# Two steps of an attention schedule in another order: the low parts of the next keys, and the weighted sums of a pair of heads

## The chip, the cores and the metric

The kernel runs on one core of one Trainium2 chip. The time is that of one launch in device microseconds (us), the median of several runs. The core's engines are called by their names in the profile: PE (TensorE, matrix products), DVE (VectorE), ACT (ScalarE), POOL (GpSimd) and SP (SyncE, which here only issues DMAs). Each of them works through its own list of instructions in order.

## The reference, cut to what matters

Three layers follow each other, and each takes the output of the one before.

```
scores = q k^T / 8                      # 4 batches x 8 heads, 576 tokens, head size 64, fp32
scores = where(block_i >= block_j, scores, -1e9)      # blocks of 64 tokens
attn   = exp(scores - rowmax);  attn /= rowsum
x      = attn v                         # then (2304 tokens, 512)

e      = argmax(x w_gate + bias[modality])            # 8 experts
x      = gate * relu(x w1[e]) w2[e]                   # 512 -> 1024 -> 512

h      = x w_in                                       # 512 -> 2048
out    = where(h >= 1, h, where(h <= -1, 0, (h+1)^2/4)) w_out
```

Everything is fp32 to a tight tolerance. A product is therefore made of several with 32-bit operands in a high and a low part: high is the rounded value, low is what the rounding left.

## The kernel before, in words

The work lies in three stretches: attention (to about 225 us of the span), experts (to about 450 us), the last layer (the rest). The change concerns attention alone.

Attention goes over 16 pairs of heads, n = 0 to 15; pair n is two heads of batch n // 4. For a pair there are seven kinds of score tiles, by rows of queries and by heads (`kinds`, line 312): kind 0 and 1 hold both heads, kinds 2 to 5 one head each, kind 6 the last 64 rows of both. A pair is seven steps, z = 0 to 6, and `orders` gives the kind of each step: for the pairs 1 to 14 the kinds 3, 1, 0, 4, 2, 6, 5, for pair 0 the kinds 2, 4, 0, 1, 5, 6, 3, and for pair 15 the kinds 3, 1, 4, 2, 6, 0, 5. The third step is z = 2, the fourth z = 3.

What a step puts into the engines' lists is written out by hand in the loop at lines 510 to 539, in this order:

- what `PLAN` has for (z, 0);
- `scores`: PE makes one tile of scores in PSUM;
- what `PLAN` has for (z, 1);
- `flip`: PE turns the exponentials of the step two before (LAG = 2), piece by piece, into a PSUM tile `pt`, and for most kinds ACT copies it to `pT` (line 388);
- `soft`: DVE takes the row maximum of the scores (lines 348, 353, 357), ACT takes the exponential with its row sum (line 359);
- DVE copies the turned tiles that ACT doesn't (kinds 1 and 6, line 523);
- what `PLAN` has for (z, 2).

The words in `PLAN`, which `act` (line 478) reads:

- "q", "k": PE turns the next pair's queries or keys into PSUM (`psq`, `psk`). For the keys DVE copies 128 columns to `kT` (line 291) and ACT writes the high parts `kd` (line 293, two instructions); POOL doubles them (line 295).
- "low": DVE computes the low parts `kl` of those keys from `psk` and `kd` (line 489, two instructions, called low below).
- a pair of numbers: `weigh`, PE's weighted sums of the values of the previous pair for these key tiles (line 402, `px`). "first": those of the first 64 rows (line 417, `py`), where for odd n - 1 DVE also lays out the row factors (lines 438 and 444), and ACT copies `py` to `xT` (line 421). "store": ACT copies `px` to `xT` (line 407), and for odd n - 1 the rows of that pair of pairs are put on the list `todo`.
- "rows": one entry of `todo`: PE turns finished rows back and multiplies them with the gate (line 454, `xr`), DVE scales them (lines 460 and 464), SP writes them to DRAM.
- "sum": DVE's reciprocal of the row sums (lines 426 and 427).

PSUM is shared: `psq`, `psk` and the scores of kind 6 use one tile ("big", one buffer), so kind 6 of a pair can be started when low has read `psk`. The turned tiles `pt`, the tile `py` and a tile `rkp` of the routing use two buffers in turn ("pt"). In the last two pairs the routing of the first 13 row tiles is woven in, up to three DVE instructions or small groups per step (lines 529 to 531).

```
PLAN = {(1, 0): ["rows", "q"], (2, 0): ["sum"], (2, 2): ["k", (0, 3)], (3, 0): ["rows"], (3, 2): ["low"],
        (4, 2): [(3, 5)], (5, 0): ["first"], (5, 1): ["store"], (6, 2): ["rows"]}
```

Of the kernel before, what the change touches and what calls it, by code (L numbers as in the profile page):

```python
# [49 lines left out]


ORDER_FIRST, ORDER_LAST, ORDER = (2, 4, 0, 1, 5, 6, 3), (3, 1, 4, 2, 6, 0, 5), (3, 1, 0, 4, 2, 6, 5)
PLAN = {(1, 0): ["rows", "q"], (2, 0): ["sum"], (2, 2): ["k", (0, 3)], (3, 0): ["rows"], (3, 2): ["low"],
        (4, 2): [(3, 5)], (5, 0): ["first"], (5, 1): ["store"], (6, 2): ["rows"]}
FROM = 0, 128, 256, 320, 448
LAG = 2
COPY = 4
# [64 lines left out]
def attention(late, weights, tc, q, k, v, ids, w_gate, mbias, x_dram, dram, ident, tabs):  # L122
# [355 lines left out]
    def act(n, z, at):  # L478

        if n >= B * NP:  # L480
            return
        for what in PLAN.get((z, at), ()):
            if what == "q" and n + 1 < B * NP:
# [1109 lines left out]
```

## Time and profile before

| | |
|---|---|
| median of 3 runs | 844.05 us (843.9 to 845.23) |
| the profiled execution | 843.12 us, span of its instructions 841.3 us |
| PE busy | 811.1 us (96% of the span) |
| DVE busy | 587.3 us (70%) |
| ACT busy | 474.9 us (56%) |
| POOL busy | 203.8 us (24%) |
| granted TensorE clock | 1.000 in the mean |

All shares are over the whole span, and the three stretches differ: from 240 us on PE is busy in every slice, and the chain of waits that ended last is nothing but PE there. In attention PE is busy for 18.0 to 19.0 of every 20 us between 40 and 180 us, and the other engines are far busier than in the rest.

### The profile page before, as it was taken

To read this page: it belongs to the slowest core of one execution; us is meant where nothing else is said; L and a number is where in the kernel's file an instruction comes from. 1 tells how busy PE (TensorE), PEld (TensorE's weight loads), DVE (VectorE), ACT (ScalarE), POOL (GpSimd) and SP (SyncE) were. 2 spreads that over 40 slices of the span, in tenths; PEclk is the share of its full clock that TensorE was granted. 3 is DMA by queue.
4 is the path that set the end of the run, shared out by engine and by line. 5 is a ranking of instruction groups with operands and counts; after the bars stand their busy time and mean duration, and the time that the engine had idled before them with its cause. 6 is when DMAs were issued, how large, how long until landed. Compare 5 with 4: busy or idle time off the path is not lost. (4 is left out here: it accounts for less than half of the span.)

```text
span 841.3 us, 13981 instructions
## 1 busy us (share of the span) xinstructions
PE 811.1 (96%) x4936; PEld 703.1 (84%) x4936; DVE 587.3 (70%) x1085; ACT 474.9 (56%) x964; POOL 203.8 (24%) x309
## 2 busy tenths in 40 slices
PE   6999999998899999999999999999999999999998
PEld 5676767766788888888888999999999988888887
DVE  6676666769666746787873766766636777777774
ACT  5867767766633434555543667666657644444442
POOL 8546455465411212120202000110000011112120
PEclk9999999999999999999999999999999999999999
DMA  6545646541654447665634453554634643333301
GB/s 144 133 123 136 169 123 160 144 100 36 214 169 125 168 121 236 224 202 163 194 115 138 142 175 125 170 180 145 206 123 161 226 147 137 126 125 126 129 35 38
DMA packets 138058, 123.17 MB, mean 146 GB/s; under 512 B 70183, under 2 KB 122423, under 8 KB 135296
## 3 DMA queue, kind: packets, MB, share of 16 engines
q1 hardware_dynamic: 132256, 107.98, 41.8%
q0 software_dynamic: 4384, 13.92, 4.8%
q8 instruction: 40, 0.66, 0.3%
q10 hardware_dynamic: 1344, 0.33, 0.2%
q14 instruction: 34, 0.28, 0.1%
HBM read 89.17 MB, written 40.37 MB: 154 GB/s over the span
## 5 line engine op out<-in xcount | busy, mean ns | idle before, releaser
L1031 PE MATMUL h<-yhi,wi 128*128 128x384 f32 x768 | 200.5, 338 | 1.1 <-ACTq L1265 1.1
L1031 PEld LDWEIGHTS h<-yhi,wi 128*128 128x128 f32 x768 | 139.6, 188 | 1.6 <-ACTq L1265 1.6
L1031 PE MATMUL h<-ylo,wi 128*128 128x384 f32 x384 | 129.2, 336 | 0.0
L359 ACT ACTIVATE pall<-s,nmax 128x384 f32<-128x384 f32 (+2 forms) x144 | 80.1, 568 | 51.2 <-DVE nmax L357 46.7
L1305 ACT ACTIVATE cl<-h,half 128x384 f32<-128x384 f32 x96 | 55.7, 581 | 69.5 <-PE h L1031 69.2
L1309 DVE SCALAR_TENSOR_TENSOR gg<-cl,h 128x384 f32<-128x384 f32 x96 | 52.2, 551 | 51.7 <-ACT cl L1306 49.7
L1435 PE MATMUL p<-wo,s 128*128 128x256 f32 (+1 forms) x432 | 87.8, 339 | 0.0
L1435 PEld LDWEIGHTS p<-wo,s 128*128 128x128 f32 x432 | 68.5, 188 | 9.2
L1490 POOL DMA_INDIRECT out_dram<-rest,tab x16 | 27.3, 1705 | 190.6 <-DVE rest L1457 185.0
L1031 PEld LDWEIGHTS h<-ylo,wi 128*128 128x128 f32 x384 | 72.1, 188 | 0.0
L377 PE MATMUL pt<-ident,pall 128*128 128x128 f32 x400 | 65.1, 281 | 3.8 <-DVE pT L523 1.8
L1435 PE MATMUL p<-wo,a 128*128 128x256 f32 (+1 forms) x330 | 66.0, 335 | 0.0
L1031 PE MATMUL h<-xhi,wh 128*128 128x512 f32 (+2 forms) x164 | 63.1, 385 | 0.0
L1031 PE MATMUL h<-xhi,wl 128*128 128x512 f32 (+2 forms) x164 | 61.6, 376 | 0.5 <-DVE wl L1115 0.5
L1031 PE MATMUL h<-xlo,wh 128*128 128x512 f32 (+2 forms) x164 | 61.6, 375 | 0.0
L1140 PE MATMUL acc<-wh,hl 128*128 128x512 f32 x152 | 59.6, 392 | 0.2 <-DVE hl L1129 0.2
L1435 PEld LDWEIGHTS p<-wo,a 128*128 128x128 f32 x330 | 52.8, 188 | 8.0
L1140 PE MATMUL acc<-wl,hh 128*128 128x512 f32 x152 | 59.3, 390 | 0.0
L1140 PE MATMUL acc<-wh,hh 128*128 128x512 f32 x152 | 59.1, 389 | 0.0
L357 DVE TENSOR_REDUCE nmax<-s 128x1 f32<-128x384 f32 (+1 forms) x64 | 39.7, 621 | 24.1 <-PE s L338 23.2
L1306 ACT ACTIVATE cl<-cl 128x384 f32<-128x384 f32 x96 | 50.5, 526 | 3.0
L1115 DVE TENSOR_TENSOR wl<-raw,wh 128x1024 fp32r<-128x1024 f32 x40 | 48.8, 1220 | 0.8 <-issue 0.8
(322 smaller groups left out, 1766.2 us busy)
## 6 DMA issues: line engine op xcount, KB each, us to landing
raw<-in_moe_w_dram SPq DMA_DIRECT2D x80, 256.0 KB
g_dram<-gg SPq DMA_DIRECT2D x48, 384.0 KB
g<-g_dram SPq DMA_DIRECT2D x18, 1024.0 KB
wi_raw<-in_moe_w_in_dram SPq DMA_DIRECT2D x16, 512.0 KB
wo_raw<-in_moe_w_out_dram SPq DMA_DIRECT2D x16, 512.0 KB
yr<-y_dram SPq DMA_DIRECT2D x18, 256.0 KB
x_dram<-xrow SPq DMA_DIRECT2D x33, 128.0 KB
v<-in_v_dram SPq DMA_DIRECT2D x32, 128.0 KB
```

The source lines that it names most:

```text
L357: nc.vector.tensor_reduce(nm[:, x:x + 1], pss, axis=AX.X, op=ALU.max, negate=True)
L359: nc.scalar.activation(pall[n % 2][:, o:o + w], pss[:, u:u + w], AF.Exp, bias=nm[:, x:x + 1], scale=1.0, accum_out=ssum[:, b, c, x:x + 1])
L377: nc.tensor.transpose(pt[:, kk, :], pa[:, o + kk * P:o + (kk + 1) * P], ident)
L1031: nc.tensor.matmul(ps, a[za], b[zb], start=(i == 0), stop=(i == n - 1))
L1115: nc.vector.tensor_tensor(wl, weights.raw.pop((s, f)), wh.bitcast(F32), op=ALU.subtract)
L1140: nc.tensor.matmul(accs[s][u], a[:, us], b[:, 1, :], start=(f == 0 and i == 0), stop=(f == NF - 1 and i == 2))
L1305: nc.scalar.activation(cl, ph, AF.Relu, bias=half, scale=0.5)
L1306: nc.scalar.activation(cl, cl, AF.Square)
L1309: nc.vector.scalar_tensor_tensor(gg[:, :, f % 2, :], cl.rearrange(t3, t=P), 1.0, ph.rearrange(t3, t=P), op0=ALU.min, op1=ALU.max)
L1435: nc.tensor.matmul(o, a, b, start=(x == 0 and i in FRESH), stop=(x == len(terms) - 1), skip_group_check=True)
L1490: outs.append(nc.gpsimd.indirect_dma_start(out=out[:, :], out_offset=bass.IndirectOffsetOnAxis(ap=tabs.tab[:, j, 0:1].bitcast(U32), axis=0 ...
```

## The change

One table is changed. Low moves from the end of the fourth step to its head, ahead of the scores and the softmax of that step. The weighted sums, which were made in three places (key tiles 0 to 2 at the end of the third step, 3 and 4 at the end of the fifth, the first 64 rows at the head of the sixth), now all stand at the end of the third step. The copies to `xT` follow at the fourth step rather than the sixth, and one of the "rows" moves from the head of the fourth step to the head of the fifth. No instruction is added or taken away.

```
-PLAN = {(1, 0): ["rows", "q"], (2, 0): ["sum"], (2, 2): ["k", (0, 3)], (3, 0): ["rows"], (3, 2): ["low"],
-        (4, 2): [(3, 5)], (5, 0): ["first"], (5, 1): ["store"], (6, 2): ["rows"]}
+PLAN = {(1, 0): ["rows", "q"], (2, 0): ["sum"], (2, 2): ["k", (0, 5), "first"], (3, 0): ["low"], (3, 1): ["store"],
+        (4, 0): ["rows"], (6, 2): ["rows"]}
```

In the lists below a name carries its pair: `s7_4` is the score tile of pair 7 and kind 4, `nmax7` its row maxima, `kl8` the low parts of the keys of pair 8, `xr` and `xrow` belong to "rows", and the last number only tells instances apart.

DVE, from the third to the sixth step of pair 7, before:

```order
L353 TENSOR_REDUCE nmax7_1488<-s7_0_1549 128x2
L291 COPY kT8_1568<-psk8_1562 128x128
L460 TENSOR_TENSOR xrow6_0_1590<-xr6_0_1587,rt_165 128x256
L464 TENSOR_TENSOR lg_166<-xr6_0_1587,rt_165 128x32
L357 TENSOR_REDUCE nmax7_1488<-s7_4_1594 128x1
L523 COPY pT7_1553<-pt7_1_0_1598 128x2x2x128
L489 TENSOR_TENSOR kl8_1570<-psk8_1562,kd8_1569 64x576 x2
L357 TENSOR_REDUCE nmax7_1488<-s7_2_1608 128x1
L348 TENSOR_REDUCE nmax7_1488<-s7_6_1626 128x1
```

and now:

```order
L353 TENSOR_REDUCE nmax7_1495<-s7_0_1556 128x2
L291 COPY kT8_1575<-psk8_1569 128x128
L489 TENSOR_TENSOR kl8_1577<-psk8_1569,kd8_1576 64x576 x2
L357 TENSOR_REDUCE nmax7_1495<-s7_4_1604 128x1
L523 COPY pT7_1560<-pt7_1_0_1609 128x2x2x128
L460 TENSOR_TENSOR xrow7_0_1620<-xr7_0_1617,rt_165 128x256
L464 TENSOR_TENSOR lg_166<-xr7_0_1617,rt_165 128x32
L357 TENSOR_REDUCE nmax7_1495<-s7_2_1624 128x1
L348 TENSOR_REDUCE nmax7_1495<-s7_6_1634 128x1
```

Low (line 489) now stands ahead of the maximum of kind 4, and the scaling of the rows behind it.

DVE in pair 0, whose fourth step is kind 1, before:

```order
L353 TENSOR_REDUCE nmax0_249<-s0_0_285 128x2
L291 COPY kT1_304<-psk1_298 128x128
L353 TENSOR_REDUCE nmax0_249<-s0_1_316 128x2
L489 TENSOR_TENSOR kl1_306<-psk1_298,kd1_305 64x576 x2
L357 TENSOR_REDUCE nmax0_249<-s0_5_333 128x1
```

and now:

```order
L353 TENSOR_REDUCE nmax0_249<-s0_0_285 128x2
L291 COPY kT1_304<-psk1_298 128x128
L489 TENSOR_TENSOR kl1_306<-psk1_298,kd1_305 64x576 x2
L353 TENSOR_REDUCE nmax0_249<-s0_1_318 128x2
L357 TENSOR_REDUCE nmax0_249<-s0_5_333 128x1
```

Here nothing but low and the maximum of kind 1 change places.

ACT in pair 14, from the third step to the sixth, before:

```order
L293 CAST kd15_2827<-psk15_2820 64x576 x2
L359 ACTIVATE pall0_157,ssum_163<-s14_4_2841,nmax14_2749 128x512
L388 COPY pT14_2810<-pt14_0_0_2877 128x2x128
L359 ACTIVATE pall0_157,ssum_163<-s14_2_2873,nmax14_2749 128x384
L421 COPY xT_162<-py13_2890 128x64
L407 COPY xT_162<-px13_2834 128x512
```

and now:

```order
L293 CAST kd15_2827<-psk15_2820 64x576 x2
L421 COPY xT_162<-py13_2845 128x64
L407 COPY xT_162<-px13_2834 128x512
L359 ACTIVATE pall0_157,ssum_163<-s14_4_2855,nmax14_2749 128x512
L388 COPY pT14_2810<-pt14_0_0_2897 128x2x128
L359 ACTIVATE pall0_157,ssum_163<-s14_2_2893,nmax14_2749 128x384
```

The two copies to `xT` now come right behind the high parts of the keys.

## Rows read from the trace of the kernel before

**Rows 1.** Page, part 2: granted clock in 40 slices, tenths of full speed

```profile
PEclk9999999999999999999999999999999999999999
```

**Rows 2.** Waits of PE, 0 to 240 us: us in total, times, longest

```profile
PE s L325 <- DVE kl L489: 15.4, 15, 1.8
```

**Rows 3.** Timeline of PE, kind 6 of pair 5: start, us, engine, line, count, idle before

```profile
84.36 0.40 PE L325 MATMUL s<-kd,qa 128*128 128x288 f32 x1 [0.99 <-DVE kl L489]
```

**Rows 4.** Timeline of PE, pair 7, fourth to seventh step

```profile
106.02 0.76 PE L454 MATMUL xr<-rh,xT 128*128 128x144 f32 x4
106.52 0.49 PE L335 MATMUL s<-kd,qa 128*128 128x512 f32 x1
...
108.34 0.66 PE L402 MATMUL px<-pT,v 128*64 128x192 f32 x8
108.83 0.29 PE L417 MATMUL py<-pT,v 128*64 128x64 f32 x4
110.10 0.40 PE L325 MATMUL s<-kd,qa 128*128 128x288 f32 x1 [0.99 <-DVE kl L489]
...
111.95 0.52 PE L377 MATMUL pt<-ident,pall 128*128 128x128 f32 x3
```

**Rows 5.** Timeline of DVE, pair 7, fourth and fifth step

```profile
106.82 0.42 DVE L460 TENSOR_TENSOR xrow<-xr,rt 128x256 f32<-128x256 f32 x1 [2.69 <-DMA q<-qc]
...
107.33 0.69 DVE L357 TENSOR_REDUCE nmax<-s 128x1 f32<-128x512 f32 x1
107.94 0.68 DVE L523 COPY pT<-pt 128x512 f32<-128x512 f32 x1
108.53 1.51 DVE L489 TENSOR_TENSOR kl<-psk,kd 64x576 fp32r<-64x576 f32 x2
110.08 0.56 DVE L357 TENSOR_REDUCE nmax<-s 128x1 f32<-128x384 f32 x1
```

**Rows 6.** Timeline of ACT, from the keys of pair 8 to those of pair 9

```profile
105.07 1.29 ACT L293 CAST kd<-psk 64x576 fp32r<-64x576 f32 x2
...
110.67 0.58 ACT L359 ACTIVATE pall<-s,nmax 128x384 f32<-128x384 f32 x1 [1.58 <-DVE nmax L357]
...
111.24 0.20 ACT L421 COPY xT<-py 128x64 f32<-128x64 f32 x1
...
111.81 0.61 ACT L388 COPY pT<-pt 128x512 f32<-128x512 f32 x1
...
114.95 0.65 ACT L252 ACTIVATE qT<-psq 128x576 f32<-128x576 f32 x1 [0.19 <-PE psq L183]
115.93 0.58 ACT L388 COPY pT<-pt 128x512 f32<-128x512 f32 x1 [0.33 <-PE pt L377]
...
118.37 1.29 ACT L293 CAST kd<-psk 64x576 fp32r<-64x576 f32 x2
```

**Rows 7.** Timeline of POOL and DVE, pair 8

```profile
116.92 2.33 POOL L262 TENSOR_TENSOR qa<-qT,qa 64x448 fp32r<-64x448 f32 x2
...
123.49 0.39 DVE L438 COPY rt<-rinv 64x16 f32<-64x16 f32 x2
```

**Rows 8.** Line 426 over the whole program: ns min/median/max, first and last start

```profile
L426 DVE TENSOR_SCALAR rinv<-ssum x8: 164/172/244, 38.4 to 222.1; 128x18 f32<-128x18 f32 x8
```

**Rows 9.** Timeline of pair 0: low, the last exponential of kind 1, its turning

```profile
18.85 1.52 DVE L489 TENSOR_TENSOR kl<-psk,kd 64x576 fp32r<-64x576 f32 x2 [0.60 <-ACT kd L293]
...
19.78 0.47 ACT L359 ACTIVATE pall<-s,nmax 128x256 f32<-128x256 f32 x1
...
21.39 0.60 PE L377 MATMUL pt<-ident,pall 128*128 128x128 f32 x4
```

**Rows 10.** Timeline of pair 14: the routing's tile, the high parts, the turning of kind 6

```profile
198.76 0.56 PE L686 MATMUL rkp<-oh,ones 128*128 128x104 bf16 x13 [0.21 <-DVE oh L678]
...
199.14 1.28 ACT L293 CAST kd<-psk 64x576 fp32r<-64x576 f32 x2
...
205.83 0.77 PE L377 MATMUL pt<-ident,pall 128*128 128x128 f32 x5 [0.54 <-ACT pall L359]
```

## The prediction

> **What bounds the kernel now.** I read the clock first: the granted share stands at nine tenths or more in all 40 slices [rows 1], which is the 2.4 GHz level, so durations can be carried from one place to another. Then the waits of PE over attention. One entry stands out: PE waits for low 15 times, 15.4 us in all, at most 1.8 [rows 2]. In the timeline that wait is 0.99 us before the first product of kind 6 in pair 5 and again in pair 7 [rows 3, 4], and 15 of them are the pairs 0 to 14, each of which prepares the keys of a next pair. The longest is that of pair 0; the other 14 share 15.4 - 1.8 = 13.6, 0.97 each.
>
> Why it waits: kind 6 needs the PSUM tile that holds the next keys, and low is the last to read it. In pair 7 low runs from 108.53 to 110.04 [rows 5], although all that it needs, the high parts, is there at 105.07 + 1.29 = 106.36 [rows 6]. In between DVE does the rows of the step, the maximum of kind 4 and a copy. So the wait is one of order on DVE, and everywhere else in these steps PE goes from one instruction to the next. Attention is PE plus this wait: two pairs take 110.10 - 84.36 = 25.74 us, 12.87 per pair, of which 11.88 is PE's own work [rows 3, 4].
>
> **The change part by part.** No instruction comes or goes, so each term is a wait.
>
> *Pairs 1 to 13, low earlier.* Low would begin at 106.40, when ACT's second high part is done, and give the tile free at 106.40 + 1.55 = 107.95 (1.55 is from its start to that of the next DVE instruction, 108.53 to 110.08 [rows 5]). PE has the same work as before between the keys and kind 6, only in another order, so it gets there at 110.10 - 0.99 = 109.11 [rows 4]. That is 1.16 us after the tile is free: the whole wait goes, 13 x 0.99 = 12.9 us. On SP the loads of values, which wait for the last weighted sum, come earlier by the same move, and nothing is queued behind them that was not before.
>
> *What is late next.* Behind low on DVE now stand the maximum of kind 4, the copy of a turned tile, the rows and the maximum of kind 2. With the sums moved ahead, PE begins kind 4 at 106.02 + (108.83 - 108.34) + 0.29 = 106.80 [rows 4] and DVE could take its maximum 0.81 later (106.52 to 107.33 [rows 4, 5]), at 107.61; low holds DVE until 107.95. Then 0.61 for the maximum, 0.59 for the copy (108.53 - 107.94), 0.51 for the rows (107.33 - 106.82), 0.59 from the maximum of kind 2 to its exponential (110.67 - 110.08) [rows 5, 6]: the exponential begins at 110.25 and ends at 110.83. PE wants it for turning kind 2 at 111.95 - 0.99 = 110.96 [rows 4]. The cover is 0.13 us, so a little will show.
>
> It can become more, since this is a ring: high parts on ACT, low, the two maxima, the exponential of kind 2, and ACT's way to the next high parts. From the start of the high parts to low it is 1.33, then 1.55 + 0.61 + 0.59 + 0.51 + 0.59 = 3.85, so 5.18. ACT's way from that exponential to the next high parts is 118.37 - 110.67 = 7.70; the two copies to xT (0.57, 111.24 to 111.81) leave it, which gives 7.13, and 0.52 of that is idle, waiting for PE (0.19 and 0.33), which gives 6.61 [rows 6]. The ring is 11.79 to 12.31 against PE's 11.88: from nothing to 0.43 us per pair, to 5.6 us in 13 pairs. I take 0.12, near the lower end, because both idle pieces wait for PE, and PE will come sooner: 1.6 us.
>
> *Row factors beside POOL.* In the pairs 2, 4, ... 12 four short DVE copies (lines 438 and 444) move from the sixth step, where POOL is done, to the third. There POOL does two subtractions, 116.92 to 119.25 in pair 8 [rows 7]. The copies take some 0.7 us (two are 0.39 [rows 7]); unhindered they are over 1.4 us before low can begin. If DVE and POOL shut each other out, each copy would get its turn only between two of POOL's instructions, the second after 119.25 and the last about 0.9 later; low would begin 0.5 late, 3.0 us in six pairs. Line 426, a short DVE instruction that runs while POOL works, takes 164 ns at best, 172 in the middle and 244 at worst [rows 8], so there is something, but small. I take 0.15 us in six pairs, 0.9 us, between nothing and 3.0. The Trainium skill, "SBUF — State Buffer", Who interferes with whom, says that a DVE copy in a two-port mode and a GpSimd instruction keep each other out for the whole of an instruction, whoever came first. By that rule the upper end holds; the spread of line 426 speaks for the rule and against its full price.
>
> *Pair 0.* Here low already waits for the high parts: 0.60 idle, released by ACT [rows 9]. It can't begin before 18.85, so the wait of 1.8 stays. But the maximum of kind 1, which ran before it, now comes after, at 18.85 + 1.55 = 20.40, and takes 0.69 as the other 512-wide one [rows 5]; two exponentials of 0.47 [rows 9] end at 22.07, and PE wants to turn kind 1 at 21.39 [rows 9]. That is 0.7 us late, and the exponential of kind 5 behind it adds about 0.2: a loss of 0.9 us (0 to 1.3, as PE has some slack later or not).
>
> *Pair 14 and the end of attention.* py now holds the buffer that the routing's tile rkp wants next, and ACT frees it only behind the high parts: 199.14 + 1.28 + 0.20 = 200.62, where PE began rkp at 198.76 [rows 10, 6]. That is a new wait of 1.9 us in PE's list, and low, the maxima and the routing queue behind it on DVE. It stands in for this pair's wait for low (under 1.0); followed to the turning of kind 6 (205.83, which waited 0.54 for ACT [rows 10]) I make it 1.2 later than before. About 0.7 comes back: one of the "rows" (0.50, 106.02 to 106.52 [rows 4]) is now done within the pairs and not between the first expert products, and pair 15 has its sums in one place. Net loss 0.5 us, from a gain of 0.7 to a loss of 1.9. Everything after 225 us hangs on this end alone and moves with it.
>
> *Sum.* -12.9 + 1.6 + 0.9 + 0.9 + 0.5 = -9.0 us. On the profiled execution, 843.12, this is 834.1; that execution lies 0.9 below the median of the runs, 844.05, from which it is 835.0. I take 834.5. All ends at their best give -13.6, all at their worst -1.1.
>
> **The rivals.**
> - *The maxima become the bound.* The ring is 12.31, since ACT keeps its idle pieces: -12.9 + 5.6 + 0.9 + 0.9 + 0.5 = -5.0, 838.6. For it: a cover of 0.13 us is no cover. Against it: both idle pieces wait for PE. 14%.
> - *Row factors shut out by POOL*, at full price: -12.9 + 1.6 + 3.0 + 0.9 + 0.5 = -6.9, 836.7. For it the 244 ns, against it the median of 172. 9%.
> - *All 15 waits go* and nothing takes their place: -15.4, 828.2. Against it are pair 0, where low is not held by order, and pair 14. 7%.
> - *It doesn't do what it says*: what PE saves in a pair is waited for elsewhere, or lost at the end of attention, where the weights of the first expert are fetched. 843.5. Against it: PE's other waits in attention are single ones. 6%.
> - *Slower.* The same ring, decided on ACT: if its way from the exponential to the high parts stays 7.70 although two copies left it, because DVE and PE pace it, the ring is 5.18 + 7.70 = 12.88, as long as a pair now. From there every further delay is a loss: with the row factors (3.0) and the pairs 0 and 14 (1.4) it is +4.4, 848. For it: low stands ahead of a maximum that ACT waits for. Against it: ACT has 1.58 us idle before this very exponential [rows 6], which is what low had put there. 7%.
>
> **How the numbers follow.** The forecast has 57%, by itself between 831.5 and 837. With the rivals that end lower or higher but faster (14, 9 and 7) faster has 87%, the same 6%, slower 7%; 0.2%, 1.7 us, is about what a measurement of this kernel can tell from no change. The range, 829 to 840, leaves out no change, slower and half of the case of all 15, some 16%.
>
> **What would show it.** Right: PE's wait for low is gone from the pairs 1 to 13 and stays at about 1.8 in pair 0; the starts of kind 6 lie 24 us apart over two pairs rather than 25.74; DVE idles before low, released by ACT's high parts; the maximum of kind 4 starts as low ends; PE waits 1 to 2 us before rkp. Wrong: a wait of several tenths in every pair before the turning of kind 2 (the ring), row factor copies that take or wait more than a few tenths (POOL), or an unchanged distance between the starts of kind 6. If attention ends 9 us earlier and the whole does not, the gain was lost behind it.

## The result, and the profile after

The changed kernel takes 834.06 us in the median of 4 runs (833.38 to 835.09), the kernel before, beside it, 843.97 (843.76 to 845.23): a ratio of 0.9876, 95% interval 0.9859 to 0.9893. Its profiled execution took 834.36 us, with a span of 832.6.

Waits of PE, 0 to 240 us, of the changed kernel (us in total, times, longest); they answer to [rows 2]:

```profile
PE pt L377 <- ACT pall L359: 4.8, 17, 0.3
...
PE pt L377 <- DVE pT L523: 2.2, 3, 1.1
PE s L325 <- DVE kl L489: 1.7, 1, 1.7
PE rkp L686 <- ACT xT L421: 1.6, 1, 1.6
```

The wait for low, 15 times before, is left once, in pair 0. The first row is largely new (it was 0.9 us in 2 before), a third of a microsecond at the turnings of most pairs, and so is the last.

PE around kind 6 of the pairs 5 and 7 (start, us, engine, line, tiles, count, idle before), against [rows 3, 4]:

```profile
80.88 0.38 PE L325 MATMUL s<-kd,qa 128*128 128x288 f32 x1
...
100.38 2.81 PE L402 MATMUL px<-pT,v 128*64 128x512 f32 x20
103.02 0.29 PE L417 MATMUL py<-pT,v 128*64 128x64 f32 x4
103.23 0.50 PE L335 MATMUL s<-kd,qa 128*128 128x512 f32 x1
...
103.81 0.20 PE L338 MATMUL s<-maskk,maskq 128*128 128x64 bf16 x1
103.85 0.63 PE L377 MATMUL pt<-ident,pall 128*128 128x128 f32 x4
...
105.20 0.41 PE L377 MATMUL pt<-ident,pall 128*128 128x128 f32 x2
105.37 0.38 PE L325 MATMUL s<-kd,qa 128*128 128x288 f32 x1
...
107.16 0.20 PE L338 MATMUL s<-maskk,maskq 128*128 128x64 bf16 x1
107.67 0.55 PE L377 MATMUL pt<-ident,pall 128*128 128x128 f32 x3 [0.31 <-ACT pall L359]
```

Kind 6 starts with no wait. From pair 5 to pair 7 it is 105.37 - 80.88 = 24.49 us instead of 25.74. The last row is the turning of kind 2, which now waits for its exponential. That wait costs more than its 0.31: after the mask product of line 338 PE goes on in 0.04 us elsewhere (103.81 to 103.85), here after 0.51 (107.16 to 107.67), so 0.47.

The chain behind it, DVE and then ACT in pair 7, against [rows 5, 6]:

```profile
103.05 1.52 DVE L489 TENSOR_TENSOR kl<-psk,kd 64x576 fp32r<-64x576 f32 x2 [2.27 <-ACT kd L293]
104.61 0.69 DVE L357 TENSOR_REDUCE nmax<-s 128x1 f32<-128x512 f32 x1
105.21 0.68 DVE L523 COPY pT<-pt 128x512 f32<-128x512 f32 x1
105.93 0.42 DVE L460 TENSOR_TENSOR xrow<-xr,rt 128x256 f32<-128x256 f32 x1
...
106.36 0.55 DVE L357 TENSOR_REDUCE nmax<-s 128x1 f32<-128x384 f32 x1
```

```profile
101.72 1.29 ACT L293 CAST kd<-psk 64x576 fp32r<-64x576 f32 x2
...
106.95 0.58 ACT L359 ACTIVATE pall<-s,nmax 128x384 f32<-128x384 f32 x1 [0.58 <-DVE nmax L357]
...
113.67 1.29 ACT L293 CAST kd<-psk 64x576 fp32r<-64x576 f32 x2
```

Low starts when ACT's high parts are there, DVE idle 2.27 us before it, and the maximum of kind 4 starts as low ends. From there DVE has no gap until the exponential of kind 2, for which PE waits. The last row is the high parts of the next pair.

Attention is read best from the starts of kind 6 (first product of line 325 in a pair), which serve for all kernels below:

| kernel | pair 1 | pair 13 | the 12 pairs between | pair 15 | first expert product |
|---|---|---|---|---|---|
| before | 32.70 | 188.45 | 155.75 | 214.47 | 227.86 |
| changed | 32.32 | 179.09 | 146.77 | 207.57 | 219.17 |

The 12 pairs give 8.98 us. At pair 13 the changed kernel is 9.36 ahead, at the first expert product 8.69, at the end of the span 841.3 - 832.6 = 8.7: nothing of it is lost behind attention.

Pair 14 is where some of it went. PE there, and windows of 2 us over the same stretch (busy us of PE, PEld, DVE, ACT and POOL, granted clock, DMA share, GB/s):

```profile
191.73 0.54 PE L686 MATMUL rkp<-oh,ones 128*128 128x104 bf16 x13 [1.59 <-ACT xT L421]
...
194.37 0.69 PE L377 MATMUL pt<-ident,pall 128*128 128x128 f32 x2 [1.09 <-DVE pT L523]
```

```profile
190.00:192.00 2.00, 0.41 (x10) 0.27 (x8) 1.40 (x5) 1.95 (x6) 1.63 (x4) 1.00 0.00 0
...
194.00:196.00 2.00, 1.63 (x7) 1.63 (x8) 1.93 (x8) 1.29 (x4) 0.00 (x0) 0.58 0.06 19
196.00:198.00 2.00, 2.00 (x11) 1.58 (x10) 1.34 (x7) 0.89 (x4) 0.23 (x1) 0.56 0.17 55
```

Before rkp PE waits 1.59 us (1.9 was forecast), soon after that 1.09 more for a copy that DVE makes behind low, and then the granted clock is 0.58 and 0.56, near the 1.2 GHz level, in the windows from 194 to 198 us. In the kernel before [rows 10], whose mean granted clock is 1.000, PE went through this place at 2.4 GHz.

### The profile page after: what moved, and what is told of

Same layout as the page of the kernel before. It is cut to its first block, busy times and chain, and to the rows that moved or that the text cites. A ratio compares the mean times of both kernels' runs of the same rounds, so it can differ in the third digit from the quotient of the medians.

```text
span 832.6 us, 14002 instructions
## 1 busy us (share of the span) xinstructions
PE 809.4 (97%) x4936; PEld 705.7 (85%) x4936; DVE 595.9 (72%) x1085; ACT 476.5 (57%) x964; POOL 204.4 (25%) x309
## 5 line engine op out<-in xcount | busy, mean ns | idle before, releaser
L377 PEld LDWEIGHTS pt<-ident,pall 128*128 128x128 f32 x400 | 43.2, 143 | 11.3 <-ACT pall L359 7.8
L1112 ACT CAST wh<-raw 128x1024 fp32r<-128x1024 f32 x40 | 41.9, 1050 | 12.6 <-PE acc L1140 12.4
```

The source lines that it names most:

```text
L377: nc.tensor.transpose(pt[:, kk, :], pa[:, o + kk * P:o + (kk + 1) * P], ident)
L1112: nc.scalar.copy(ws[s, f][0], weights.raw[s, f])
```

## The experiments

Chips differ by some tenths of a per cent (the kernel before takes 843.97, 841.43, 844.9 or 841.29 us), so each kernel's ratio is to the kernel before on its own chip. The ranges in the expectations are in microseconds and do not follow the chip, so it is the trace first that tells the theories apart.

**Low alone.** Against the kernel before:

```
-... (3, 0): ["rows"], (3, 2): ["low"], ...
+... (3, 0): ["low", "rows"], ...
```

> Only low is moved, to the head of the fourth step (ahead of the rows that stand there); the weighted sums, first, store and rows stay where they were before. Theory A (a ring through DVE and ACT bounds the changed kernel, and taking ACT's two copies to xT out of ACT's way is half of the change): PE's wait for low goes in the pairs 1 to 13, but the copies to xT (about 0.5 us) are back between the exponential of kind 2 and the next high parts, so the turning of kind 2 or a later one waits some 0.6 to 0.9 us in every pair: 838 to 842 us. Theory B (PE's wait for low was everything, the sums were moved for nothing): the 12.9 us go and little comes back, and pair 14 keeps its old order: 830 to 833 us.

Measured: 843.03 us against 841.43, ratio 1.0017 (1.0008 to 1.0026). The move that removes 13 waits of a microsecond gains nothing by itself. Its waits of PE, then PE and DVE in pair 10:

```profile
PE py L417 <- DVE pT L523: 9.7, 13, 0.8
```

```profile
146.44 0.42 PE L377 MATMUL pt<-ident,pall 128*128 128x128 f32 x2
146.79 0.66 PE L402 MATMUL px<-pT,v 128*64 128x192 f32 x8
148.23 0.34 PE L417 MATMUL py<-pT,v 128*64 128x64 f32 x4 [0.79 <-DVE pT L523]
```

```profile
145.33 1.52 DVE L489 TENSOR_TENSOR kl<-psk,kd 64x576 fp32r<-64x576 f32 x2 [2.27 <-ACT kd L293]
146.89 0.69 DVE L357 TENSOR_REDUCE nmax<-s 128x1 f32<-128x512 f32 x1
147.50 0.68 DVE L523 COPY pT<-pt 128x512 f32<-128x512 f32 x1
```

py takes the PSUM buffer of the turned tile that DVE copies, and that copy now stands behind low and the maximum. The wait moved from one reader of DVE's list to the next. Both theories missed. A, by which most of the wait comes back, was nearer, but with the wrong cause: not ACT's copies, a shared buffer. The 12 pairs gain 2.09 us (155.75 to 153.66), and pair 14, where one turning waits 3.40 us for DVE, takes them back.

**The sums alone.** Against the changed kernel:

```
-... (3, 0): ["low"], (3, 1): ["store"], ...
+... (3, 1): ["store"], (3, 2): ["low"], ...
```

> Low stays behind the maximum of kind 4 as before; the sums of a pair in one stretch, first, store and rows as in the changed kernel. Theory A (PE waits from the scores of kind 4 to low, 3.54 us by the order on DVE, whatever stands between on PE): the wait for low grows to 1.2 to 1.4 us, since the last two sums no longer fill it and one rows does; PE's own work is about 0.2 us per pair shorter for the one stretch; with the wait for rkp in pair 14 it comes out at 845 to 849 us. Theory B (the one stretch is a gain by itself, 0.2 us in 13 pairs, and the wait for low stays 0.99): 841 to 842 us.

Measured: 844.81 against 841.43, ratio 1.0044 (1.0030 to 1.0058). The time is 0.2 us below theory A's range, the wait is theory A's: for low it is 19.4 us in 15, so (19.4 - 1.8) / 14 = 1.26 each instead of 0.97:

```profile
PE s L325 <- DVE kl L489: 19.4, 15, 1.8
```

So neither half is a gain, and the two together are 1.2%: the early low needs py out of the buffer's way, and the early sums need low out of PE's.

**Both, the sums in two pieces.** Against the changed kernel:

```
-... (2, 2): ["k", (0, 5), "first"], (3, 0): ["low"], (3, 1): ["store"], (4, 0): ["rows"], ...
+... (2, 2): ["k", (0, 3), "first"], (3, 0): ["low"], (4, 0): ["rows"], (4, 2): [(3, 5)], (5, 1): ["store"], ...
```

> The changed kernel with the sums split again (three of five at the third step, two at the fifth) and store back at the sixth; first (py) stays early, low early. Low alone gained nothing because PE's wait moved from low to py, which takes the PSUM buffer of the turned tile that DVE copies behind low (9.7 us in 13 pairs). Theory A (py's place is what the second half of the change is for): no wait of py, and only the dearer split, some 0.2 us per pair, and the copy to xT on ACT's way are lost: 835 to 837.5 us. Theory B (the one stretch of sums and the early store carry the gain, as ACT's copies stand in the ring again): 839 to 842 us, with waits of 0.7 us before the turnings.

Measured: 839.3 against 844.9, ratio 0.9934 (0.9916 to 0.9953). The time is at theory B's edge; the ratio, at 843.97 for the kernel before, gives 838.4, between the two. In the pairs the mechanism is theory A's: py waits no more, the sums cost more in two pieces, the 12 pairs take 149.42 us, 2.65 more than in the changed kernel, and the waits before the turnings are 0.2 to 0.3 us with one of 0.74, not 0.7 each. The rest is lost in the pairs 14 and 15, which neither theory had: PE waits 2.0 us for rkp and twice some 1.6 us for DVE's copies. The split on PE in pair 13:

```profile
176.77 2.37 PE L402 MATMUL px<-pT,v 128*64 128x512 f32 x12
178.97 0.28 PE L417 MATMUL py<-pT,v 128*64 128x64 f32 x4
...
181.15 0.42 PE L377 MATMUL pt<-ident,pall 128*128 128x128 f32 x2
181.50 0.66 PE L402 MATMUL px<-pT,v 128*64 128x192 f32 x8
182.09 0.40 PE L325 MATMUL s<-kd,qa 128*128 128x288 f32 x1
```

Two pieces take 178.97 - 176.77 = 2.20 us and, with the turning ahead, 182.09 - 181.15 = 0.94; in one stretch, with the same turning, it is 103.02 - 100.38 = 2.64 and 105.37 - 105.20 = 0.17. So the one stretch saves 3.14 - 2.81 = 0.33 us of PE per pair. The Trainium skill, "TensorEngine Tiling (Array Packing)", Key Properties, says that a change of tiling mode drains the engine: the sums are 128*64 in these rows, their neighbours 128*128, and a split adds a change each way. The rows agree in direction, with no fixed price: two turnings take 0.35 ahead of sums and 0.17 ahead of scores.

**Rows behind the maximum of kind 2.** Against the changed kernel:

```
-        (4, 0): ["rows"], (6, 2): ["rows"]}
+        (4, 2): ["rows"], (6, 2): ["rows"]}
```

> The changed kernel with the rows of the fifth step moved behind the scores and the maximum of kind 2 (from the head of the fifth step to its end). Theory A (the remaining 0.3 us before the turning of kind 2 is the ring of high parts, low, maximum, copy, rows, maximum and exponential): the rows' 0.44 us leave it, the wait of 0.3 us goes in most pairs and the starts of kind 6 come some 0.3 us closer in every pair: 829.5 to 831.5 us. Theory B (ACT and PE pace the ring, DVE's part has room): no change, 833.5 to 834.5 us, the same waits of 0.3 us.

Measured: 829.38 against 841.43, ratio 0.9856 (0.9836 to 0.9876), theory A, with a time 0.1 us below its range. The 12 pairs take 142.32 us, 4.45 less than in the changed kernel, and PE's waits for exponentials there fall from 15 to 5. So the exponential of kind 2 was the end of a ring through DVE.

**Pair 14 in the old order.** Against the changed kernel, where `PLAN_14` is the whole table of before:

```
-        for what in PLAN.get((z, at), ()):
+        for what in (PLAN_14 if n == 14 else PLAN).get((z, at), ()):
```

> The changed kernel, but in pair 14 alone the old order (sums in two pieces, first and store at the sixth step, low behind the maximum of kind 4). Theory A (what pair 14 lost is the wait for rkp, 1.59 us, with the turning behind it, 1.09 us, and the half clock granted to PE after them, about 1.2 us, against 0.74 us for low there): the wait before rkp falls to about 0.2 us, the granted clock stays 1.00 between 190 and 200 us, and the time falls by 1.5 to 2.5 us, to 831.5 to 832.5. Theory B (pair 15 takes it back, as it took 1.8 us back in the changed kernel): 833.5 to 834.5 us although the wait goes.

Measured: 832.37 against 841.43, ratio 0.9896 (0.9881 to 0.9911). PE in pair 14 (lines stand two further on):

```profile
189.67 0.56 PE L688 MATMUL rkp<-oh,ones 128*128 128x104 bf16 x13 [0.24 <-DVE oh L680]
191.06 0.44 PE L379 MATMUL pt<-ident,pall 128*128 128x128 f32 x2 [0.19 <-DVE pT L525]
192.94 0.40 PE L327 MATMUL s<-kd,qa 128*128 128x288 f32 x1 [0.73 <-DVE kl L491]
```

The waits are as forecast, and the granted clock is 1.00 in every window from 188 to 200 us. The first expert product comes at 217.20 instead of 219.17. By the time this is not told from the changed kernel, whose ratio is 0.9876 and, in a later run, 0.9897; the trace alone shows it.

**Late rows, and pair 14 in the old order**, both edits together:

> The rows at the end of the fifth step, and in pair 14 alone the old order. Theory A (the two gains lie in different places, 4.7 us in the pairs and 1.7 us in pair 14, which here has waits of 1.6 and 1.6 us and 6 us at half clock): they add up, 826.5 to 828 us, granted clock 1.00 throughout attention. Theory B (what pair 14 gives is taken back behind it, where PE now waits 1.1 us for a gather): 828.5 to 829.5 us.

Measured: 828.28 against 844.9, ratio 0.9807 (0.9784 to 0.9830), between the two ranges. The 12 pairs take 142.10 us, the first expert product is at 213.00 (215.81 with the late rows alone). The gains lie in different places and add up in the trace. The granted clock is 1.00 in pair 14, but not throughout attention as theory A has it: it is 0.50 to 0.69 from 8 to 16 us, and 0.52 and 0.63 from 22 to 26 us, behind kind 6 of pair 0.

**Late rows, and another buffer for py in pair 14:**

```
-        if n < B * NP - 1:
+        if n not in (13, B * NP - 1):
             px = ps1.tile([P, 512], F32, tag="pt", name=f"py{n}", bufs=4 - SB)
```

> The rows at the end of the fifth step, and py of pair 13 alone (weighed in pair 14) in a PSUM buffer of the other tag, so that rkp need not wait for ACT's copy; low stays early in pair 14. Theory A (the wait for rkp is a wait for py's buffer): it falls from 1.6 us to some tenths, the wait of the turning of kind 4 behind it stays at 1.0 to 1.6 us, since low still stands ahead of DVE's copy: 827 to 828.5 us. Theory B (DVE's list, not the buffer, sets pair 14): rkp starts earlier and the turning waits that much longer, 829 to 830 us.

Measured: 832.14 against 844.9, ratio 0.9844 (0.9823 to 0.9866), above both ranges and no better than the late rows alone. rkp waits no more, the turning behind it waits the longer, which is theory B's mechanism:

```profile
189.32 0.44 PE L377 MATMUL pt<-ident,pall 128*128 128x128 f32 x2 [3.34 <-DVE pT L523]
```

In pair 14 it is DVE's list with low ahead of the copy that is late, not the buffer.

**Late rows, and the row factors late too** (the copies of lines 438 and 444, three in most pairs, leave the third step):

```
-        (4, 2): ["rows"], (6, 2): ["rows"]}
+        (4, 2): ["order", "rows"], (6, 2): ["rows"]}
...
+            elif what == "order":
+                if (n - 1) % 2:
+                    row_order((n - 1) // NP, (n - 1) % NP // 2)
```

> The rows at the end of the fifth step, and the four short copies of row factors directly ahead of them instead of at the third step beside POOL's subtraction. In the changed kernel they take 2.1 us there in place of 0.7, and low still starts only when ACT's high parts are done, 0.34 us after them. Theory A (that cover hides them): the distances between the starts of kind 6 stay at 11.56 and 11.95 us, DVE's idle time before low grows from 0.34 to above 2 us in the pairs with copies: 828.5 to 830 us. Theory B (their length costs something all the same): the pairs with copies get 0.1 to 0.5 us shorter, 826 to 828.5 us.

Measured, one run: 835.15 us; both theories missed. Line 438 over the program in the changed kernel, then here (ns min/median/max, first and last start, forms):

```profile
L438 DVE COPY rt<-rinv x12: 174/710/1166, 39.7 to 214.7; 64x16 f32<-64x16 f32 x8, 128x16 f32<-128x16 f32 x4
```

```profile
L438 DVE COPY rt<-rinv x12: 176/178/183, 45.0 to 212.6; 64x16 f32<-64x16 f32 x8, 128x16 f32<-128x16 f32 x4
```

DVE and ACT of this kernel in pair 12:

```profile
164.86 0.55 DVE L357 TENSOR_REDUCE nmax<-s 128x1 f32<-128x384 f32 x1
165.44 0.18 DVE L438 COPY rt<-rinv 128x16 f32<-128x16 f32 x1
165.53 0.33 DVE L444 COPY rt<-rinv 64x2 f32<-64x2 f32 x2
165.89 0.42 DVE L460 TENSOR_TENSOR xrow<-xr,rt 128x256 f32<-128x256 f32 x1
```

```profile
167.11 0.74 ACT L359 ACTIVATE pall<-s,nmax 128x576 f32<-128x576 f32 x1 [0.52 <-DVE nmax L348]
```

Away from POOL the copies are short, 0.45 us together, and cost all of it: they stand ahead of the maximum of kind 6, ACT waits for that, and from pair 12 to 13 it is 12.39 us rather than 11.96. Beside POOL they are four to five times as long and nearly free, because low waits for ACT longer than for them.

**Rows one step later still, and pair 14 old**, run beside the kernel of the late rows with pair 14 old and the changed kernel:

```
-        (4, 2): ["rows"], (6, 2): ["rows"]}
+        (5, 2): ["rows"], (6, 2): ["rows"]}
```

> As the run with the late rows and the old order in pair 14, but the rows stand one step later still, behind the maximum of kind 6. There PE still waited 0.38 us in every second pair before the turning of kind 6. Theory A (the rows ahead of the maximum of kind 6 are what is late): that wait goes, the distance of 11.95 us falls to some 11.6, and with six such pairs the time is 1.5 to 2.5 us below that of the kernel with the rows at the end of the fifth step, run beside it. Theory B (PE's own work is the bound by now, or the wait comes from ACT's list): within 0.7 us of it.

> The late rows with the old order in pair 14, word for word as run before, now beside the changed kernel. If the two gains add up (4.7 us in the pairs, 2 in pair 14, by the starts of kind 6), it lies 5.5 to 7 us below the changed kernel; if what pair 14 gives is lost again, 4 to 5 us.

> The changed kernel, word for word, on the chip of the two others. It should lie 9 to 11 us below the kernel before.

| on one chip, before 841.29 | us | ratio | 95% |
|---|---|---|---|
| changed kernel | 833.02 | 0.9897 | 0.9882 to 0.9913 |
| late rows, pair 14 old | 827.34 | 0.9827 | 0.9813 to 0.9840 |
| rows one step later, pair 14 old | 829.99 | 0.9864 | 0.9849 to 0.9879 |

The changed kernel lies 8.3 us below before, a little less than expected; the best version 5.7 below the changed kernel, as if the gains add up. One step later is too late. The wait before the turning of kind 6 is gone from the pairs 3 to 13, but the product for the rows no longer stands on PE ahead of the turning of kind 4, which now waits in all of the pairs 1 to 13 but one (below in pair 11). From an even pair to the next it is 12.34 us instead of 11.95, from an odd one 11.44 to 11.84 instead of 11.56. Both theories missed.

```profile
153.90 0.65 PE L379 MATMUL pt<-ident,pall 128*128 128x128 f32 x4 [0.24 <-ACT pall L361]
```

## Why the prediction came out right

The time, 834.06, is within half a microsecond of the 834.5 forecast. By its own terms that is partly luck: two errors cancel.

- *The wait for low goes in the pairs 1 to 13* (-12.9): right. It is gone in all of them, and DVE idles before low, released by the high parts.
- *PE has the same work as before, only in another order*: this step failed. In one stretch the sums take 0.33 us less per pair, 4.3 us in 13, a gain the sum did not have. The kernel before shows the same 3.14 for its two pieces, 106.02 - 103.72 = 2.30 [rows 4] and, with the turning ahead, 108.83 - 107.99 = 0.84:

```profile
103.72 2.37 PE L402 MATMUL px<-pT,v 128*64 128x512 f32 x12
...
107.99 0.41 PE L377 MATMUL pt<-ident,pall 128*128 128x128 f32 x2
```

  An edit that only moves matmuls was costed at nothing because their number stayed.
- *What is late next* (+1.6, up to 5.6): right in place, too small. 15 waits for exponentials lie in the 12 pairs, 4.7 us as shown; with the 0.16 each that the rows don't show (0.47 against 0.31) 7.1 us, about 0.6 per pair instead of 0.12. The DVE part was right: from the end of low to the exponential 2.30 us forecast, 106.95 - 104.61 = 2.34 measured. The ring has the forecast length: from the high parts to the exponential 106.95 - 101.72 = 5.23 (5.18 forecast), from there to the next high parts 113.67 - 106.95 = 6.72 (6.61 to 7.13 forecast), 11.95 in all. From an odd pair to the next kind 6 comes after 11.94 us in the changed kernel, in three of five cases also with the sums in two pieces, although PE's work is longer there, and after 11.56 once the rows' 0.43 us leave the ring. So the rival of the maxima was nearer in mechanism than in time. What the ring was held against was too long, for two reasons. PE's work is the 0.33 shorter: without its wait PE would stand at the turning 107.67 - 0.47 - 101.72 = 5.48 us after the start of the high parts, where the working had 110.96 - 105.07 = 5.89 [rows 4, 6], and the cover of 0.13 was gone. And 11.88 is the mean of unequal pairs. In the kernel before, the start in pair 6

```profile
96.80 0.40 PE L325 MATMUL s<-kd,qa 128*128 128x288 f32 x1 [0.99 <-DVE kl L489]
```

  gives PE's own work as 96.80 - 84.36 - 0.99 = 11.45 us from an odd pair to the next and 110.10 - 96.80 - 0.99 = 12.31 from an even one [rows 3, 4]. In the odd pairs even the shortest ring of the forecast, 11.79, is longer than that.
- *Net of the two*, per 12 pairs: 12 x 0.99 and one wait of 0.3 go, 12.2; 7.1 come; 12 x 0.33 = 4.0 go; 9.1, against 8.98 measured. The 0.99 is idle time as shown too. By the starts it is 1.06: from py to the next product it is 0.21 in the changed kernel (103.02 to 103.23) and 110.10 - 108.83 = 1.27 before [rows 4]. So what came is nearer 8 us than 7.1.
- *Row factors beside POOL* (+0.9): the lengthening came, the cost did not. Only the pairs 6 and 8 have four copies, the others have three. The four take 2.4 us in pair 8, beside line 262 of POOL:

```profile
112.29 2.33 POOL L262 TENSOR_TENSOR qa<-qT,qa 64x448 fp32r<-64x448 f32 x2
...
112.76 1.91 DVE L438 COPY rt<-rinv 64x16 f32<-64x16 f32 x2
...
114.69 0.46 DVE L444 COPY rt<-rinv 64x2 f32<-64x2 f32 x2
115.16 1.52 DVE L489 TENSOR_TENSOR kl<-psk,kd 64x576 fp32r<-64x576 f32 x2
```

  Low follows them without a gap there, about 0.16 late, and so in pair 6; in the four pairs with three copies it still waits 0.34 for ACT. So some 0.3 us. At its upper end the working let the last copies end 0.9 us after POOL's subtractions; they end 0.53 after them (115.15 against 114.62). By the rule of the Trainium skill that the prediction weighed ("SBUF — State Buffer", Who interferes with whom) they shut each other out: the trace agrees, 710 ns in the median where 179 stood before. The spread of line 426 [rows 8] was no measure of it.
- *Pair 0* (+0.9): nearly right. The wait for low stays (1.67). As idle time only 0.21 and 0.11 show before two turnings behind it, but from kind 6 to the turning of the next queries (line 185) the same work takes 24.92 - 20.79 = 4.13 us instead of 23.91 - 20.52 = 3.39, 0.74 more.
- *Pair 14 and the end* (+0.5): 9.36 ahead at pair 13, 8.69 at the first expert product, so +0.67. The wait before rkp was seen (1.59), the second wait and the half clock were not; 1.8 us came back behind kind 6 of pair 15, more than the 0.7 forecast.

Of the tests named for "right", all came out, except that the distance over two pairs is 24.2 to 25.1 instead of 24. Two of the signs named for "wrong" are there as well: a wait of several tenths before the turning of kind 2 in most pairs (the ring), and row factor copies that take 1.8 to 2.4 us instead of 0.7 (POOL).

## What to carry to other kernels

Where an early instruction removes a wait, look at what now stands behind it on its engine and ask who reads each of those: low alone removed 13 us of waits and gained nothing. A place beside a rival engine can be the cheap one if something else is awaited there anyway; the copies cost more where they were shorter. And an instruction that no one awaits soon (the rows) belongs behind the last maximum that someone does, but no further than where its product on PE still fills time in which PE would wait. And a ring is to be held against the shortest of the pairs that it runs through, not against their mean.

## What the runs showed of the hardware

- Sums on 128*64 tiles cost 0.33 us of PE more per pair when split in two among 128*128 work (3.14 against 2.81).
- The granted clock fell after PE's waits of 1.59 and 1.09 us with 1.55 us between them (0.58 and 0.56 in the changed kernel), and after one of 3.34 (0.67, then 0.50). It stayed at 1.00 through 0.24, 0.19 and 0.73 in pair 14 in the old order. The length of a wait alone does not tell it: with the sums in two pieces it stayed at 1.00 after 1.67 us in pair 0 and was 0.56 and 0.59 in the windows from 218 to 222 us, after 1.67 us in pair 15. From kind 6 of pair 14 to the mask product behind the next scores, 194.71 to 197.89, PE took 3.18 us in the changed kernel; the same products took 1.78 in pair 11 at full clock.
